# A fused attention and Mish kernel: its head written into the step list, and its first loads cut differently

## The chip, the cores and the metric

The kernel runs on one core of one Trainium2 chip. The metric is device time in microseconds (us), the median of several executions. A core has five engines that run side by side and wait for each other through semaphores: TensorE (PE; its weight loads are listed as PEld) multiplies matrices into PSUM, VectorE (DVE), ScalarE (ACT) and GpSimd (POOL) compute elementwise, and SyncE (SP) issues transfers. ScalarE can issue transfers too. In the profile, "SPq" and "ACTq" are issues of transfers. A program for this core is one list of instructions per engine, each executed in the order in which the kernel's code issued them.

## The reference, cut to what matters

```python
x  = A_x                              # 1 x 2048 x 512, bf16
xn = layernorm(x)                     # over the last axis, no scale or shift
# A: linear attention, 32 heads of 16
q, k, v = split(xn @ wqkv)
pq, pk = q @ w_phi[h], k @ w_phi[h]   # per head, 16 x 16
phi(p) = concat(softmax(p), softmax(-p))
kv = sum_s phi(pk)[s] x v[s];   z = sum_s phi(pk)[s]
o = (phi(pq) @ kv) / (phi(pq) . z + 1e-6)
# B: an MLP
h = xn @ w1 + b1                      # 512 -> 1792
B = (h * tanh(softplus(h))) @ w2      # Mish, 1792 -> 512
out = x + o @ wo + B
```

## The kernel before

The 2048 rows are 16 tiles of 128, in four groups of four. All of x, of the normalised and transposed xn (`xnT`), and of the activated hidden layer (`acts`) stay in SBUF.

The work is cut into named steps, and the order in which the steps are issued is written out by hand in the string `PLAN` (lines 20 to 76). `step(name)` (line 606) takes a name such as `unit_0_7` apart and issues its instructions. So `PLAN` sets the order on every engine at once. A trailing number of some steps picks the engine: for copies out of PSUM (names that end in `=`) 0 is ScalarE and 1 VectorE; for `apply` 0 is VectorE and 2 ScalarE; for `sums` 0 is VectorE and 1 GpSimd. What the names mean:

- `spread_t` (L184), `gather_g` (L189), `root_g` (L202 to L207, GpSimd): statistics of tile t, mean and variance of group g, and 1/sqrt of the variance. `apply_t` (L219, L224) normalises tile t. `turned_t` (L240) turns tiles t and t+1 by a transposing DMA from SP into `xnT`.
- `value_t` and `logits_s_i` (L250, four 128x512 matmuls each): tile t times the value weights; tile i of group s times the folded key weights `wkp` (s below 4) or query weights `wqp` (s from 4 on). Their copies out of PSUM are `value=`, `logits=` and, for the negated query logits, `minus=`. `fold_j` (L164) is a block of the weight product wqkv x w_phi, from `wT`, the transposed weight that a DMA brings (`wq`, L158), and `Wbd`, w_phi as a block diagonal (L550).
- `plane_s_p` (L336 to L344, VectorE): the logits of group s less their row maximum (p = 0) or minimum less the logits (p = 1), both needed before `exp_s_i` (L353, ScalarE); `sums` (L363, L367), `normal_s_k` (L409 to L414, tiles 2k and 2k+1) finish the softmaxes of the keys; `add_s_i` (L427, eight matmuls of 66 columns) sums phi(k) x v; `kv` masks the total. `shift`, `weigh`, `turn`, `attend`, `divide`, `out` do the same for the queries, with DMA transposes (`turn`, `out`).
- `unit_g_f` (L265, four matmuls): block f of the hidden layer for group g; `unit=` (L275) is its Mish on ScalarE, straight from PSUM. It needs `b1f`, the bias turned by TensorE.
- `second_t_n`, `project_t` (L500, L509), `residual_t` (L517), `store_t`: the second layer, the output projection, the sum with x and the store.
- `w2`, `wo`, `wq`: loads of weights.

PSUM has eight banks of 128x512 fp32. `bank(name)` (L125) hands out a bank in turn from a pool; a bank is given again when the step that read it is done. Pool `ps` has six. In the head the function alternates between `ps` and a second pool `hd` of two banks, which is closed behind the head; the two banks later hold the sum of `add`, and then the results of `attend`.

In front of `PLAN` stands the head, written out in lines 524 to 599. The loads are issued first (L524 to L533): on SP tiles 0 and 1 of x, the transposed key weight, tiles 4 to 7, the value weights, all of w1, tiles 8 to 15; on ScalarE's queue w_phi, tiles 2 and 3, the bias. GpSimd builds the identity and the masks. TensorE runs eleven warming matmuls on the identity. Then, for group 0, the statistics come tile by tile, with the square root on ScalarE (`deviate`, L194) and the reciprocal on VectorE (`invert`, L198); TensorE turns the four tiles (`turn_pe`, L233), folds the key weights (L164), and multiplies (L250). Everything of the head is issued before the first step of `PLAN`, `spread_4`; the engines run from the one into the other without a stop.

Of the kernel before, what the change touches and what calls it, by code (L numbers as in the profile page):

```python
# [22 lines left out]
unit_0_5 spread_9 unit=_0_11 spread_11 unit_0_1 unit=_0_5 apply_7_0 apply_6_0 apply_4_2 unit_0_0
spread_10 turned_6 unit=_0_1 unit_0_6 apply_5_0 plane_0_1 unit=_0_0 turned_4 unit_0_9 unit=_0_6
unit_0_10 unit=_0_9 value_0 unit=_0_10 w2 gather_2 value_7 spread_15 root_2 spread_12 logits_1_2
exp_0_2 value=_0_1 value_6 spread_13 exp_0_3 logits_1_0 apply_8_0 apply_11_0 exp_0_0 apply_9_0
unit_0_4 apply_10_0 turned_8 value=_7_1 sums_0_2_1 logits=_1_2_0 unit_1_4 value=_6_0 sums_0_0_0
turned_10 exp_0_1 logits_1_1 gather_3 logits_1_3 logits=_1_0_0 sums_0_1_0 unit_0_2 root_3 sums_0_3_0
value_5 unit=_0_4 unit=_1_4 normal_0_0 unit_1_9 unit=_0_2 unit_2_1 logits=_1_1_0 logits=_1_3_0
unit_2_5 unit=_1_9 apply_12_0 unit_1_6 value=_5_0 plane_1_0 apply_15_2 add_0_0 unit_2_0 apply_14_2  # L30
logits_2_2 unit=_1_6 turned_14 unit=_2_1 unit_1_13 plane_1_1 logits=_2_2_0 wo unit=_2_5 unit_2_3
unit=_1_13 add_0_1 logits_2_1 unit=_2_3 unit=_2_0 value_4 normal_0_1 value_11 exp_1_3 logits_2_3
logits_2_0 apply_13_2 logits=_2_1_1 sums_1_3_1 exp_1_0 add_0_3 turned_12 value=_4_1 add_0_2 unit_1_8
value=_11_1 exp_1_2 logits=_2_0_1 unit_2_12 exp_1_1 sums_1_0_0 value_10 sums_1_2_1 logits=_2_3_0
sums_1_1_0 unit_1_10 unit_1_7 normal_1_0 unit=_1_8 unit_1_5 unit=_2_12 unit_0_13 value=_10_0
unit=_1_7 unit_1_1 plane_2_0 unit=_1_10 unit_2_4 unit=_1_1 unit=_0_13 unit_2_10 unit=_1_5 unit_1_11
unit=_2_10 plane_2_1 unit=_2_4 unit_3_2 wq unit=_1_11 unit_3_5 unit=_3_2 logits_3_1 unit=_3_5
logits_3_3 normal_1_1 add_1_0 logits_3_2 exp_2_2 logits_3_0 exp_2_1 logits=_3_1_1 unit_3_4
logits=_3_0_0 sums_2_1_1 logits=_3_2_1 exp_2_3 unit_3_0 sums_2_2_0 unit_1_0 logits=_3_3_0 sums_2_3_0
exp_2_0 add_1_1 add_1_3 unit_0_8 masks sums_2_0_0 value_15 normal_2_1 unit=_3_4 add_1_2 unit_2_9  # L40
unit=_3_0 unit=_1_0 unit_3_10 unit=_0_8 value_14 value=_15_0 plane_3_0 unit=_2_9 value_8 value=_14_0
add_2_2 value=_8_0 unit_3_11 unit=_3_10 fold_0 unit=_3_11 fold_3 fold_1 unit_2_13 plane_3_1
fold=_0_0 fold=_3_0 unit_1_3 unit=_2_13 unit_0_12 fold=_1_0 unit=_1_3 value_9 unit=_0_12 normal_2_0
fold_2 value_12 value_13 exp_3_3 unit_3_9 value=_9_1 exp_3_1 sums_3_3_1 value=_12_1 unit_3_6
fold=_2_1 exp_3_2 add_2_3 add_2_0 add_2_1 exp_3_0 sums_3_2_0 unit_2_11 unit_2_6 sums_3_1_1
value=_13_1 sums_3_0_0 unit_3_8 unit=_3_9 unit_1_2 unit=_2_6 normal_3_1 unit=_3_6 logits_4_1
unit=_2_11 unit_3_3 logits=_4_1_0 unit=_3_8 logits_4_0 minus=_4_1_1 unit=_1_2 normal_3_0 unit_3_12
logits=_4_0_0 unit_2_7 unit=_3_12 minus=_4_0_0 unit_2_2 unit=_3_3 shift_4_0 logits_5_3 unit=_2_2
unit=_2_7 logits_4_3 logits=_5_3_0 logits_4_2 logits=_4_3_0 logits_5_2 logits=_4_2_1 minus=_5_3_1
add_3_0 add_3_3 exp_4_0 add_3_2 add_3_1 unit_3_13 exp_4_1 kv sums_4_0_1 unit_1_12 logits=_5_2_0  # L50
sums_4_1_0 minus=_4_3_0 logits_5_0 minus=_5_2_0 minus=_4_2_1 unit_3_1 weigh_0 unit_3_7 unit=_3_13
logits_6_1 logits=_5_0_0 shift_4_1 turn_0_0 unit=_1_12 logits_5_1 minus=_5_0_0 logits_6_0 turn_0_1
logits=_6_1_0 unit=_3_1 logits_6_2 unit=_3_7 shift_5_1 logits_6_3 minus=_6_1_0 logits=_5_1_0
unit_2_8 logits=_6_2_0 logits=_6_0_0 second_0_0 minus=_5_1_0 minus=_6_0_0 shift_5_0 second_1_0
exp_4_3 attend_0_0 second_0_1 exp_4_2 divide_0_0 sums_4_3_1 minus=_6_2_0 logits_7_3 logits=_6_3_0
sums_4_2_0 out_0_0 attend_0_1 minus=_6_3_0 logits_7_0 divide_0_1 second_1_1 weigh_1 out_0_1
unit=_2_8 logits_7_1 shift_6_1 turn_1_0 second_2_0 exp_5_2 turn_1_1 exp_5_1 project_0 exp_5_0
second_2_1 residual_0 sums_5_1_1 exp_6_2 sums_5_0_0 project_1 attend_1_0 residual_1 logits_7_2
divide_1_0 store_1 second_3_0 logits=_7_2_0 weigh_2 logits=_7_3_0 out_1_0 minus=_7_3_0 attend_1_1
second_3_1 exp_6_3 shift_6_0 turn_2_1 logits=_7_0_0 second_4_0 minus=_7_0_0 turn_2_0 logits=_7_1_0  # L60
exp_5_3 second_5_0 divide_1_1 minus=_7_2_0 sums_5_3_1 exp_6_1 sums_5_2_0 project_2 out_1_1
minus=_7_1_0 second_5_1 residual_2 shift_7_1 attend_2_1 second_7_0 project_3 weigh_3 second_8_0
exp_7_2 exp_6_0 second_4_1 divide_2_1 turn_3_0 sums_6_0_1 residual_3 turn_3_1 attend_2_0 second_9_0
divide_2_0 sums_6_3_0 out_2_0 second_10_0 sums_6_2_1 sums_6_1_0 store_0 attend_3_0 store_3
second_7_1 divide_3_0 out_2_1 weigh_4 attend_3_1 store_2 project_4 out_3_0 second_9_1 residual_4
turn_4_0 weigh_5 project_5 turn_4_1 divide_3_1 second_8_1 turn_5_1 shift_7_0 second_6_0 turn_5_0
attend_4_0 second_6_1 out_3_1 residual_5 exp_7_1 divide_4_0 second_10_1 exp_7_3 sums_7_1_1 out_4_0
exp_7_0 attend_4_1 project_6 divide_4_1 second_14_0 sums_7_0_0 out_4_1 sums_7_3_1 attend_5_0 weigh_6
project_7 second_14_1 residual_7 turn_6_0 project_8 sums_7_2_1 divide_5_0 second_12_0 turn_6_1
residual_8 attend_5_1 out_5_0 project_9 divide_5_1 second_11_0 weigh_7 out_5_1 attend_6_0  # L70
second_11_1 residual_9 turn_7_1 divide_6_0 second_13_0 store_8 turn_7_0 project_10 out_6_0
attend_6_1 project_11 divide_6_1 second_12_1 residual_10 out_6_1 residual_6 attend_7_0 store_10
second_13_1 divide_7_0 store_4 out_7_0 project_12 attend_7_1 store_6 project_13 divide_7_1 store_9
second_15_0 store_7 residual_13 out_7_1 project_14 store_5 store_13 second_15_1 residual_14
# [5 lines left out]
def kernel(  # L80
# [148 lines left out]
    def turn_pe(t, copy):  # L229
        xn, i = xn_of[0], t  # L230
        ptr = bank("ptr", BF16)
        for kt in range(KT):
            nc.tensor.transpose(  # L233
                ptr[:, kt * P : (kt + 1) * P], xn[:, i, kt * P : (kt + 1) * P], ident[:]
            )
# [326 lines left out]
    for _ in range(11):
        nc.tensor.matmul(
            warm[:].rearrange("p (k c) -> p k c", k=4), lhsT=ident[:], rhs=ident[:, None, :].to_broadcast([P, 4, P]),
            start=True, stop=True,
        )

    for t in (0, 1):
        spread(t)
        gather(t, 1)  # L570
        deviate(t, 1)
    for t in (0, 1):
        invert(t, 1)
        apply(t, nc.vector)
    turn_pe(0, act)
    spread(2)
    spread(3)
    gather(2, 2)
    for kt in (0, 1):
        act(wkp[:, kt, :], fold(wT, kt)[:])  # L580
    deviate(2, 2)
    for kt in (2, 3):
        (dve if kt == 2 else act)(wkp[:, kt, :], fold(wT, kt)[:])
    turn_pe(1, dve)
    invert(2, 2)
    apply(2, nc.vector)
    apply(3, nc.vector)
    logits_copy(0, 0, project(wkp, 0), act)
    p1 = project(wkp, 1, kts=range(0, 2))
    turn_pe(2, dve)  # L590
# [126 lines left out]
```

## Time and profile before

| what | value |
|---|---|
| time, three runs | 177.01, 177.47, 177.53 us; median 177.47 |
| the profiled execution's own time | 177.59 us |
| its span on the core | 175.8 us |
| TensorE's last matmul ends | 172.2 us |
| ScalarE's table loads | 15 of 1.28 us (seven for exp, seven for Mish, one in the head) |
| instructions | 2806 |

The page gives each engine's busy time, a strip of 40 slices of the span (each digit tenths of a slice), and the chain of waits, which is followed back from the last instruction: at each step to what released it. Other views are lists of waits, a timeline (start, duration, engine, line, operation, result and operands, count, and in brackets the idle time in front and what ended it), and the transfers of a window by queue (q1 is SP's, q10 ScalarE's; packets, MB, share of the 16 transfer engines). A busy matmul row contains the time in which its results drain, so rows of neighbours overlap; what a matmul costs in a row of many is the distance of the starts. Some matmul records are missing from a trace, so counts in rows can be lower than what was issued.

### The profile page before, as it was taken

The page shows a single profiled execution, that of the slowest core. Times are in us where ns is not written, and L with a number is a line of the kernel's source. Part 1 is how long each engine was busy: PE and PEld are TensorE (multiplying, and loading weights), DVE is VectorE, ACT ScalarE, POOL GpSimd, SP SyncE. Part 2 cuts the span into 40 slices and gives each one's busy share as a digit, 9 for nine tenths or more (in the row PEclk, how much of TensorE's full clock was granted, in tenths as well). Part 3 has the DMA queues.
Part 4 walks back from the last instruction along what each step waited for, and adds up shares of the span by engine and source line. Part 5 has one row for each costly group of instructions (what it writes and reads, how often), then busy time and mean ns, then how long its engine had stood idle before and what let it go on. Part 6 is the DMA issues. An engine that isn't in the chain of part 4 may idle for free.

```text
span 175.8 us, 2806 instructions
## 1 busy us (share of the span) xinstructions
PE 168.4 (96%) x1021; PEld 82.3 (47%) x1038; DVE 151.6 (86%) x265; ACT 117.3 (67%) x168; POOL 49.3 (28%) x95
## 2 busy tenths in 40 slices
PE   6999987999999999999999999999999999999992
PEld 2444433444544454545445445444445444454571
DVE  0987899999999999998997999999998997973563
ACT  3667999898999899999999999969340006000000
POOL 4201217300550072028005006060528007910000
PEclk9999999999999999999999999999999999999999
DMA  5998089607260000000000311435616584556565
GB/s 145 285 407 305 0 173 355 129 14 171 47 132 0 0 4 0 0 2 4 0 0 0 78 45 30 91 88 127 58 28 148 141 200 85 83 126 163 130 130 179
DMA packets 44618, 18.03 MB, mean 103 GB/s; under 512 B 37052, under 2 KB 44092, under 8 KB 44604
## 3 DMA queue, kind: packets, MB, share of 16 engines
q1 hardware_dynamic: 43632, 17.50, 40.3%
q10 hardware_dynamic: 972, 0.35, 0.8%
q8 instruction: 8, 0.13, 0.3%
q14 instruction: 6, 0.05, 0.1%
HBM read 6.84 MB, written 2.10 MB: 51 GB/s over the span
## 4 chain that ended last, share of the span: by engine, by line
PE 80%; DVE 7%; DMA 7%; SPq 3%; issue 1%
PE po L500 27%; PE ph L265 22%; PE pproj L250 18%; PE po L509 8%; DMA x_sb<-in_A_x_dram 7%; DVE stats L184 2%; PE pkv L427 2%; PE pnd L464 2%; DVE xn L224 2%; SPq L158 2%; DVE m L336 1%; DVE e L344 1%; DVE vext L257 1%; PE pfold L164 1%; DVE x_sb L517 0%
## 5 line engine op out<-in xcount | busy, mean ns | idle before, releaser
L265 PE MATMUL ph<-xnT,w_sb 128*128 128x512 bf16 x224 | 51.6, 379 | 0.0
L500 PE MATMUL po<-w_sb,acts 128*128 128x512 bf16 (+1 forms) x231 | 51.3, 366 | 0.3
L353 ACT ACTIVATE e<-e 128x1024 bf16<-128x1024 bf16 x28 | 28.2, 1051 | 18.2 <-DVE e L323 18.2
L275 ACT ACTIVATE acts<-ph,b1f 128x512 bf16<-128x512 f32 x56 | 35.7, 694 | 1.6 <-PE ph L265 1.2
L367 POOL TENSOR_TENSOR t<-e 128x512 f32<-128x512 bf16 x13 | 15.4, 1187 | 68.2 <-ACT e L353 68.2
L500 PEld LDWEIGHTS <-acts 128*128 128x128 bf16 x238 | 22.7, 98 | 23.6
L265 PEld LDWEIGHTS <-w_sb 128*128 128x128 bf16 x224 | 21.3, 98 | 24.8 <-DMA w_sb<-in_B_w_dram 0.4
L250 PE MATMUL pproj<-wkv,xnT 128*128 128x512 bf16 x121 | 30.2, 379 | 2.0 <-DVE vext L257 1.2
L250 PEld LDWEIGHTS <-xnT 128*128 128x128 bf16 x192 | 18.1, 98 | 23.5 <-issue 2.2
L363 DVE TENSOR_REDUCE sums<-e 128x64 f32<-128x1024 bf16 x15 | 17.9, 1209 | 1.2 <-ACT e L353 1.2
L367 POOL TENSOR_TENSOR t<-t 128x256 f32<-128x256 f32 (+1 forms) x30 | 16.9, 564 | 2.3
L509 PE MATMUL po<-wqk,ob 128*128 128x512 bf16 (+1 forms) x67 | 16.4, 366 | 0.1
L250 PE MATMUL pproj<-wqk,xnT 128*128 128x512 bf16 x62 | 15.3, 379 | 0.1
L184 DVE BATCH_NORM_STATS2 stats<-x_sb 128x6 f32<-128x512 bf16 x16 | 10.2, 679 | 5.3 <-DMA x_sb<-in_A_x_dram 5.3
L517 DVE TENSOR_TENSOR x_sb<-po,x_sb 128x512 bf16<-128x512 f32 (+1 forms) x17 | 10.9, 654 | 2.0 <-PE po L509 1.9
L479 DVE RECIPROCAL r<-pnd 128x32 f32<-128x32 f32 x16 | 5.6, 352 | 7.3 <-PE pnd L464 7.3
L480 DVE TENSOR_TENSOR ob<-pnd,r 128x512 bf16<-128x512 f32 x16 | 11.1, 691 | 0.6
L414 DVE TENSOR_TENSOR e<-e,r 128x2048 bf16<-128x2048 bf16 x8 | 9.8, 1225 | 0.3
L353 ACT ACT_TABLE_LOAD x7 | 9.0, 1283 | 0.7 <-DVE e L323 0.3
L275 ACT ACT_TABLE_LOAD x7 | 9.0, 1283 | 0.1
L509 PEld LDWEIGHTS <-ob 128*128 128x128 bf16 x68 | 6.0, 97 | 5.9 <-DMA ob<-ob 0.5
L285 ACT CAST p<-pproj 128x512 bf16<-128x512 f32 x12 | 6.8, 579 | 2.2 <-PE pproj L250 2.2
(79 smaller groups left out, 184.4 us busy)
## 6 DMA issues: line engine op xcount, KB each, us to landing
w_sb<-in_B_w_dram SPq DMA_DIRECT2D x2, 1792.0 KB, 8.6
out_dram<-x_sb SPq DMA_DIRECT2D x15, 128.0 KB, 1.8
x_sb<-in_A_x_dram SPq DMA_DIRECT2D x1, 1024.0 KB, 11.6
x_sb<-in_A_x_dram SPq DMA_DIRECT2D x1, 512.0 KB, 4.1
wkv<-in_A_wqkv_dram SPq DMA_DIRECT2D x1, 512.0 KB, 4.7
wqk<-in_A_wo_dram SPq DMA_DIRECT2D x1, 512.0 KB, 4.0
x_sb<-in_A_x_dram SPq DMA_DIRECT2D x1, 256.0 KB, 3.1
x_sb<-in_A_x_dram ACTq DMA_DIRECT2D x1, 256.0 KB, 3.5
```

The source lines that it names most:

```text
L184: nc.vector.bn_stats(ln_of[g][0][:, t % TPG, :], x_sb[:, t, :])
L250: nc.tensor.matmul(pp, lhsT=xnT[:, t, kt, :], rhs=w[:, kt, :], start=(kt == 0), stop=(kt == KT - 1),)
L265: nc.tensor.matmul(ph[:], lhsT=w1_sb[:, kt, f * P : (f + 1) * P], rhs=xnT[:, g * TPG : (g + 1) * TPG, kt, :], start=(kt == 0), stop=(kt == ...
L275: nc.scalar.activation(acts[:, f, g * 512 : (g + 1) * 512], ph[:], ACT.Mish, bias=b1f[:, f : f + 1])
L353: nc.scalar.activation(v, v, ACT.Exp)
L363: nc.vector.reduce_sum(out, part, axis=AX.X)
L367: nc.gpsimd.tensor_tensor(out=to[:], in0=part[:, :, 0:n], in1=part[:, :, n : 2 * n], op=ALU.add)
L414: nc.vector.tensor_tensor(out=vv, in0=vv, in1=r2[:, :, None, :].to_broadcast([P, 128, 8, 2]), op=ALU.mult)
L480: nc.vector.tensor_tensor(out=o_t.rearrange("p (u v g d) -> p u v g d", u=2, v=4, g=4), in0=nd[:, :, :, 0:64].rearrange("p u v (g d) -> p ...
L500: nc.tensor.matmul(po[:, c], lhsT=acts[:, f, t * P : (t + 1) * P], rhs=w2_sb[:, f, c], start=(f == 0), stop=False,)
L509: nc.tensor.matmul(po[:, c], lhsT=oT_of[h][:, 2 + t % 2, j * P : (j + 1) * P], rhs=wo_sb[:, j, c], start=False, stop=(j == 3),)
L517: nc.vector.tensor_tensor(out=y, in0=po[:, c], in1=y, op=ALU.add)
```

## The change

The head is no longer written out behind the loads. Its parts become steps (`mean`, `deviate`, `invert`, `flip`, `foldk`, `first`, `bias` and their copies), and `PLAN` is replaced by another order in which they stand among all the others: 577 steps instead of 521, with the same work in total; `first_i_kt` is one matmul of tile i, so four of them make up a tile's logits of group 0. The new order also picks other engines for some steps: of the key logits' copies 11 are on ScalarE and 5 on VectorE (12 and 4 before, the head's included), of the folded key weights' copies all four on ScalarE (three before), of the query logits' copies 14 and 2 (15 and 1), of the `sums` 18 on VectorE and 14 on GpSimd (17 and 15). The places where ScalarE goes from exp to Mish or back, at each of which it loads a table, are 10 instead of 14.

The second PSUM pool of the head is gone: all of it uses the six banks of `ps`. The warming matmuls are nine instead of eleven. The loads: SP brings tile 0 of x alone and then the transposed key weight; ScalarE's queue brings tiles 1 to 3 in one transfer first, then w_phi and the bias; w1 comes in two halves of 896 columns (blocks 0 to 6 and 7 to 13).

The diff, cut to its core; of the plans, the beginning of the old one and the first part and the last lines of the new one:

```diff
 PLAN = """
-spread_4 spread_7 spread_6 value_3 spread_5 plane_0_0 value_1 value_2 value=_1_0 value=_3_0
-value=_2_0 unit_0_7 gather_1 unit_0_3 root_1 spread_8 unit=_0_7 unit_0_11 spread_14 unit=_0_3
...
+spread_0 mean_0 spread_3 deviate_0_1 spread_2 mean_3 mean_2 spread_1 deviate_2_2 invert_0_1
+invert_2_2 mean_1 apply_3_0 deviate_1_1 foldk_0 foldk_1 apply_2_0 foldk=_0_0 flip_3 invert_1_1
+flip_2 apply_0_0 foldk_2 foldk=_1_0 flip=_3_1 flip_0 foldk_3 apply_1_0 flip=_2_0 first_3_0 flip=_0_1
+flip_1 foldk=_2_0 first_2_0 spread_7 first_3_1 flip=_1_0 first_2_1 spread_6 first_3_2 first_0_0
+foldk=_3_0 first_1_0 spread_4 first_0_1 first_2_2 first_1_1 spread_5 first_3_3 first_1_2
+logits=_0_3_0 bias first_0_2 gather_1 first_1_3 first_0_3 root_1 logits=_0_1_1 first_2_3
+logits=_0_0_0 value_2 bias= logits=_0_2_1 unit_0_3 value=_2_1 unit_0_6 unit=_0_3 apply_6_0 apply_4_0
+apply_7_2 unit_0_5 plane_0_0 apply_5_2 turned_6 unit_0_10 unit=_0_5 value_1 unit=_0_10 turned_4
+unit=_0_6 unit_0_12 plane_0_1 unit_0_11 unit=_0_12 value=_1_0 value_3 w2 unit=_0_11 logits_1_2
+value=_3_0 value_7 spread_9 spread_12 value_4 exp_0_2 spread_11 logits_1_0 spread_10 logits=_1_2_0
+sums_0_2_1 spread_14 value_6 value=_7_0 spread_15 value=_4_0 logits_1_1 exp_0_0 spread_8 logits_1_3
+gather_2 logits=_1_0_0 sums_0_0_0 value=_6_0 root_2 value_0 exp_0_1 spread_13 unit_1_12
+logits=_1_3_1 exp_0_3 unit_1_4 gather_3 sums_0_1_0 logits=_1_1_0 root_3 unit_1_11 value=_0_0
+sums_0_3_0 unit_0_8 unit_1_1 unit=_1_12 apply_12_0 apply_8_0 unit_1_8 unit=_1_4 apply_9_0 apply_10_0
+turned_8 unit=_0_8 apply_11_0 unit_1_9 apply_14_0 unit=_1_11 plane_1_0 unit_0_7 unit=_1_8 wo
+unit=_1_1 unit_0_1 turned_10 apply_15_2 unit_1_0 unit=_0_7 turned_14 unit_1_7 unit=_1_9 normal_0_0
+unit=_0_1 unit_1_3 unit=_1_7 unit_1_6 unit=_1_0 apply_13_2 unit_1_13 plane_1_1 unit=_1_6 turned_12
+logits_2_1 unit=_1_3 unit=_1_13 add_0_0 value_5 logits_2_3 normal_0_1 exp_1_2 logits_2_0
+logits=_2_1_0 add_0_1 logits_3_2 logits=_2_3_0 exp_1_1 logits=_2_0_1 sums_1_2_1 logits_2_2
+value=_5_0 add_0_2 logits=_2_2_1 add_0_3 exp_1_0 unit_3_12 sums_1_1_0 unit_3_9 exp_1_3 sums_1_0_0
...
+divide_7_0 residual_11 out_7_0 project_12 attend_7_1 store_9 project_13 divide_7_1 store_11
+second_15_0 store_2 out_7_1 project_14 store_7 second_15_1 residual_14 residual_13 residual_12
+store_13 project_15 store_12 store_14 residual_15 store_15
 """
...
-    turns = [cycle([ps])]
-
+    
     def bank(name, dtype=FP32):
-        return next(turns[0]).tile([P, 512], dtype, name=name, tag="mm")
+        return ps.tile([P, 512], dtype, name=name, tag="mm")
...
-    nc.sync.dma_start(x_sb[:, 0:2, :], x_v[:, 0:2, :])
+    nc.sync.dma_start(x_sb[:, 0, :], x_v[:, 0, :])
+    held = {"wT": load_turned(D)}
+    nc.scalar.dma_start(x_sb[:, 1:4, :], x_v[:, 1:4, :])
     with nc.allow_non_contiguous_dma(reason="tiny w_phi load"):
         nc.scalar.dma_start(wsrc[:], wphi_v)
-    wT = load_turned(D)
-    nc.scalar.dma_start(x_sb[:, 2:4, :], x_v[:, 2:4, :])
     nc.scalar.dma_start(b1b[:], b1_v[:, :])
     nc.sync.dma_start(x_sb[:, 4:8, :], x_v[:, 4:8, :])
     nc.sync.dma_start(wv, wqkv_v[:, :, 2 * D : 3 * D])
-    nc.sync.dma_start(w1_sb[:], w1_v[:, :, :])
+    for c in (slice(0, F // 2), slice(F // 2, F)):
+        nc.sync.dma_start(w1_sb[:, :, c], w1_v[:, :, c])
     nc.sync.dma_start(x_sb[:, 8:16, :], x_v[:, 8:16, :])
...
     warm = bank("warm")
-    for _ in range(11):
+    for _ in range(9):
...
+        elif kind == "mean":
+            gather(n[0], 1)
+        elif kind == "deviate":
+            deviate(*n)
+        elif kind == "invert":
+            invert(*n)
+        elif kind == "flip":
+            held[key] = turn_pe(*n)
+        elif kind == "flip=":
+            copies[alt](xnT[:, n[0], :, :], held.pop(key))
+        elif kind == "foldk":
+            held[key] = fold(held["wT"], *n)
+        elif kind == "foldk=":
+            copies[alt](wkp[:, n[0], :], held.pop(key)[:])
+        elif kind == "first":
+            i, kt = n
+            held["logits", 0, i] = project(wkp, i, held.get(("logits", 0, i)), range(kt, kt + 1))
```

More of the change, by code (lines that the diff above doesn't have):

```diff
@@ L20 @@
 PLAN = """
-spread_4 spread_7 spread_6 value_3 spread_5 plane_0_0 value_1 value_2 value=_1_0 value=_3_0
-value=_2_0 unit_0_7 gather_1 unit_0_3 root_1 spread_8 unit=_0_7 unit_0_11 spread_14 unit=_0_3
[L23 to L74, printed above, removed]
@@ L75 @@
-residual_11 residual_12 store_11 project_15 store_14 store_12 residual_15 store_15
+spread_0 mean_0 spread_3 deviate_0_1 spread_2 mean_3 mean_2 spread_1 deviate_2_2 invert_0_1
[3 more added lines that the diff above has]
+foldk=_3_0 first_1_0 spread_4 first_0_1 first_2_2 first_1_1 spread_5 first_3_3 first_1_2
@@ new lines @@
+logits_2_1 unit=_1_3 unit=_1_13 add_0_0 value_5 logits_2_3 normal_0_1 exp_1_2 logits_2_0
+logits=_2_1_0 add_0_1 logits_3_2 logits=_2_3_0 exp_1_1 logits=_2_0_1 sums_1_2_1 logits_2_2
+value=_5_0 add_0_2 logits=_2_2_1 add_0_3 exp_1_0 unit_3_12 sums_1_1_0 unit_3_9 exp_1_3 sums_1_0_0
+masks unit_1_5 logits=_3_2_0 sums_1_3_0 unit_1_2 unit_3_1 normal_1_0 unit=_3_12 wq unit=_3_9
+unit_0_0 unit=_1_5 unit_2_11 unit=_3_1 logits_3_1 unit=_1_2 plane_2_0 unit_0_4 logits=_3_1_0
+unit=_2_11 logits_3_3 unit=_0_0 unit_2_9 unit=_0_4 normal_1_1 logits_3_0 unit=_2_9 logits=_3_3_0
@@ new lines @@
+add_1_0 unit_1_10 unit_2_6 plane_2_1 unit=_1_10 unit_2_2 unit=_2_6 logits=_3_0_0 add_1_2 fold_1
+unit=_2_2 add_1_3 fold_2 add_1_1 fold=_2_0 fold_3 unit_2_3 plane_3_0 fold=_1_0 fold=_3_0 unit_0_2
+unit=_2_3 unit_2_8 unit=_0_2 unit_3_13 unit=_2_8 plane_3_1 value_14 unit=_3_13 value_8 value_12
+exp_2_3 value_13 value=_12_1 exp_2_1 sums_2_3_1 value=_14_1 value_9 value=_13_1 exp_2_2 value_10
+value=_8_1 exp_3_3 value_15 sums_2_2_0 value=_9_0 fold_0 sums_2_1_1 value_11 exp_2_0 fold=_0_1
+value=_10_1 unit_3_6 value=_15_0 normal_2_1 exp_3_1 unit_3_5 unit_0_13 exp_3_2 unit_3_0 exp_3_0
@@ new lines @@
+value=_11_1 unit_3_2 sums_3_0_1 sums_2_0_0 add_2_2 unit_2_13 unit=_3_6 normal_2_0 add_2_3 unit=_3_5
+unit_3_7 unit=_0_13 unit_2_1 unit=_3_0 unit=_2_13 logits_4_2 unit=_3_2 sums_3_1_0 sums_3_2_1 add_2_1
+unit=_3_7 logits_4_1 unit=_2_1 sums_3_3_0 add_2_0 unit_3_8 logits=_4_2_0 normal_3_0 logits=_4_1_0
+logits_4_3 unit=_3_8 logits_4_0 logits=_4_3_0 minus=_4_2_0 unit_3_3 logits=_4_0_0 normal_3_1
+unit_2_5 minus=_4_1_0 unit=_3_3 unit_2_0 minus=_4_3_0 minus=_4_0_0 unit_2_10 unit=_2_5 shift_4_0
+unit_3_10 unit=_2_0 unit=_2_10 unit_3_11 unit=_3_10 add_3_0 unit=_3_11 add_3_3 logits_5_1 shift_4_1
@@ new lines @@
+logits_5_3 exp_4_0 add_3_1 add_3_2 logits_5_2 exp_4_1 unit_3_4 logits=_5_3_1 logits=_5_1_0
+sums_4_1_1 unit_2_4 exp_4_2 minus=_5_1_1 logits=_5_2_1 unit_2_7 exp_4_3 minus=_5_3_1 unit_0_9
+minus=_5_2_1 sums_4_2_1 sums_4_0_0 unit_2_12 unit=_3_4 logits_6_2 sums_4_3_0 unit=_2_4 logits_6_3
+unit=_0_9 weigh_0 unit=_2_7 logits_6_0 logits=_6_2_0 logits_6_1 logits=_6_3_0 weigh_1 turn_0_1
+unit=_2_12 logits_5_0 minus=_6_2_0 minus=_6_3_0 turn_0_0 logits_7_1 kv logits=_6_0_0 logits_7_0
+minus=_6_0_0 turn_1_0 shift_5_1 logits=_5_0_0 second_0_0 logits=_6_1_0 turn_1_1 minus=_6_1_0
@@ new lines @@
+attend_0_1 minus=_5_0_0 logits_7_2 divide_0_1 second_0_1 exp_5_3 shift_6_0 second_1_0 logits=_7_1_0
+minus=_7_1_0 attend_0_0 second_2_0 divide_0_0 exp_6_0 second_1_1 shift_5_0 logits=_7_0_0 out_0_0
+logits=_7_2_0 minus=_7_0_0 attend_1_0 out_0_1 logits_7_3 second_3_0 logits=_7_3_0 shift_6_1 exp_5_2
+project_0 exp_6_1 second_3_1 exp_5_0 residual_0 exp_5_1 sums_5_0_1 second_2_1 divide_1_0
+minus=_7_2_0 exp_6_2 sums_5_1_0 out_1_0 project_1 exp_6_3 attend_1_1 sums_6_0_0 second_4_0
+sums_6_1_1 minus=_7_3_0 residual_1 second_5_0 weigh_2 project_2 divide_1_1 turn_2_0 sums_5_2_1
@@ new lines @@
+second_5_1 residual_2 out_1_1 sums_5_3_0 second_7_0 turn_2_1 weigh_3 second_6_0 shift_7_0 turn_3_1
+second_4_1 turn_3_0 attend_2_0 second_8_0 store_0 divide_2_0 exp_7_1 project_3 weigh_4 exp_7_0
+out_2_0 second_6_1 sums_6_3_0 sums_7_0_1 turn_4_1 attend_2_1 second_8_1 divide_2_1 second_7_1
+residual_3 out_2_1 sums_6_2_0 sums_7_1_1 turn_4_0 attend_3_1 project_4 divide_3_1 second_9_0
+residual_4 out_3_1 attend_3_0 store_3 second_9_1 divide_3_0 weigh_5 out_3_0 project_5 attend_4_0
+second_10_0 residual_5 turn_5_0 divide_4_0 second_11_0 weigh_6 out_4_0 attend_4_1 turn_5_1 project_6
@@ new lines @@
+divide_4_1 second_11_1 store_5 shift_7_1 turn_6_0 attend_5_0 project_7 out_4_1 second_10_1 turn_6_1
+divide_5_0 exp_7_3 project_8 residual_7 exp_7_2 out_5_0 attend_5_1 residual_8 second_13_0 sums_7_2_1
+divide_5_1 project_9 sums_7_3_0 out_5_1 attend_6_0 second_13_1 residual_6 divide_6_0 store_6 store_8
+project_10 weigh_7 store_4 store_1 second_14_0 turn_7_0 second_12_0 turn_7_1 attend_6_1 second_12_1
+divide_6_1 out_6_0 residual_10 out_6_1 project_11 residual_9 attend_7_0 second_14_1 store_10
@@ L227, in apply, with turn_pe @@
         )
-    def turn_pe(t, copy):
-        xn, i = xn_of[0], t
+    def turn_pe(t):
         ptr = bank("ptr", BF16)
@@ L233, in turn_pe @@
             nc.tensor.transpose(
-                ptr[:, kt * P : (kt + 1) * P], xn[:, i, kt * P : (kt + 1) * P], ident[:]
+                ptr[:, kt * P : (kt + 1) * P], xn_of[0][:, t, kt * P : (kt + 1) * P], ident[:]
             )
-        copy(xnT[:, t, :, :], ptr[:].rearrange("p (k c) -> p k c", k=KT))
+        return ptr[:].rearrange("p (k c) -> p k c", k=KT)
     def turn_dma(t):
@@ L556 @@
     dve, act = nc.vector.tensor_copy, nc.scalar.copy
-    head = ExitStack()
-    hd = head.enter_context(tc.tile_pool(name="hd", bufs=2, space=PSUM))
-    turns[0] = cycle([hd, ps, ps, ps, hd, ps, ps, ps])
     warm = bank("warm")
-    for _ in range(11):
+    for _ in range(9):
         nc.tensor.matmul(
@@ L566 @@
         )
[L568 to L590, printed above, removed]
-    logits_copy(0, 1, project(wkp, 1, p1, kts=range(2, 4)), act)
-    turn_pe(3, act)
-    pb = bank("pb", BF16)
-    nc.tensor.transpose(pb[:, 0:FT], b1b[:], ident[0:FT, 0:FT])
-    nc.vector.tensor_copy(b1f[:], pb[:, 0:FT])
-    for i in range(2, TPG):
-        logits_copy(0, i, project(wkp, i), act)
-    head.close()
-    turns[0] = cycle([ps])
     kvp = ExitStack()
     later = []
-    held = {}
     copies, sides = (act, dve), (nc.vector, nc.gpsimd, nc.scalar)
@@ L608, in step @@
         kind, *n = name.split("_")
-        alt = int(n.pop()) if kind in ("apply", "value=", "logits=", "fold=", "sums", "minus=") else 0
+        alt = int(n.pop()) if kind in ("apply", "value=", "logits=", "fold=", "sums", "minus=", "flip=", "foldk=") else 0
         n = tuple(int(c) for c in n)
@@ L613, in step @@
             spread(*n)
+        elif kind == "mean":
[15 more added lines that the diff above has]
+            held["logits", 0, i] = project(wkp, i, held.get(("logits", 0, i)), range(kt, kt + 1))
+        elif kind == "bias":
+            held[key] = bank("pb", BF16)
+            nc.tensor.transpose(held[key][:, 0:FT], b1b[:], ident[0:FT, 0:FT])
+        elif kind == "bias=":
+            nc.vector.tensor_copy(b1f[:], held.pop(key)[:, 0:FT])
         elif kind == "gather":
```

## The prediction

> **What bounds the kernel now.** I read the page's busy rows and slices first, then the chain of waits, then the list of TensorE's waits, then the timeline of the first 50 us. The page and the chain:
>
> ```profile
> PE 168.4 (96%) x1021; PEld 82.3 (47%) x1038; DVE 151.6 (86%) x265; ACT 117.3 (67%) x168; POOL 49.3 (28%) x95
> ...
> PE   6999987999999999999999999999999999999992
> ...
> 49.44 8.63 PE ph L265 x40
> ...
> 171.73 0.47 PE po L509 x4
> 172.20 0.03 issue
> 172.23 0.42 DVE x_sb L517
> ```
>
> TensorE is the bound. From 31 to 172.2 us the chain is nearly all TensorE; only slices 5 and 6 (22 to 31 us) and the ends are not full. Forty 512-column matmuls take 8.63 us, so one takes 0.216 us. TensorE's waits and the rows around them:
>
> ```profile
> PE warm L563 <- POOL eps L537: 1.4, 1, 1.4
> PE pproj L250 <- DVE vext L257: 1.2, 1, 1.2
> PE pproj L250 <- DMA xnT<-xn: 0.4, 1, 0.4
> PE pfold L164 <- DMA wT<-in_A_wqkv_dram: 0.2, 1, 0.2
> ```
>
> ```profile
> 1.43 4.82 PE L563 MATMUL warm<-ident 128*128 128x512 bf16 x11 [1.43 <-POOL eps L537]
> 6.22 0.40 PE L233 MATMUL ptr<-ident,xn 128*128 128x128 bf16 x4
> 6.87 1.07 PE L164 MATMUL pfold<-Wbd,wT 128*128 128x128 bf16 x16 [0.25 <-DMA wT<-in_A_wqkv_dram]
> ...
> 15.23 7.94 PE L265 MATMUL ph<-xnT,w_sb 128*128 128x512 bf16 x36
> ...
> 24.43 3.63 PE L250 MATMUL pproj<-wkv,xnT 128*128 128x512 bf16 x16 [0.40 <-DMA xnT<-xn]
> 27.89 1.89 PE L265 MATMUL ph<-xnT,w_sb 128*128 128x512 bf16 x8
> 30.99 1.89 PE L250 MATMUL pproj<-wkv,xnT 128*128 128x512 bf16 x8 [1.21 <-DVE vext L257]
> ```
>
> By start times with 0.216 us for each matmul: value_0 should have ended at 23.88, the next group starts at 24.43 (0.55 lost); the eight matmuls from 27.89 end at 29.62, the next start is 30.99 (1.37 lost). That is 1.9 us of waiting in the body. The first projections (logits of group 0) end three value tiles before 15.23: 15.23 - 12 x 0.216 = 12.64.
>
> **TensorE's work behind that point** is the same steps in both plans: units 224 x 0.216 = 48.4; second layer 48.4 (the 256-column ones at half); output projection 13.8; values 64 x 0.216 = 13.8; logits of the other seven groups 112 x 0.216 = 24.2; 16 `add` and 16 `attend` at 0.256 ("0.51 pkv x16" in the chain) 8.2; query folds 0.9. Sum 157.7. Check: 12.64 + 157.7 + 1.9 = 172.2, where the chain leaves TensorE; 3.6 us of last addition and store follow, 175.8, the span. The profiled run took 177.59, 1.79 more; the median shown, 177.47, is 0.12 below it. So the time on the median's scale is (end of first projections) + 157.7 + (later waits W) + 3.6 + 1.67, and the change can move only the first term, W, and the tail.
>
> **Head, part by part.** (1) *Loads.* In the windows of the DMA view the SP queue moved 211 packets of 1 KB by 3.0 us and the ACT queue's first packets come after 2.5:
>
> ```profile
> q1 hardware_dynamic: 115, 0.12, 72.9%
> q10 hardware_dynamic: 66, 0.00, 7.2%
> ...
> 3.96 0.69 DVE L184 BATCH_NORM_STATS2 stats<-x_sb 128x6 f32<-128x512 bf16 x1 [3.96 <-DMA x_sb<-in_A_x_dram]
> ```
>
> (the two queue rows are the window 2.5 to 3.0). Tile 0 alone is 128 packets, so it is here at about 3.2 instead of 3.96. Tiles 1 to 3 (384 KB) start 0.52 us earlier on ACT's queue than tiles 2 and 3 did, which landed at 1.32 + 3.5 = 4.8; I take 4.5, bounds 4.2 and 5.0. w_phi goes second on ACT, behind 384 KB: landing 5.0 to 5.3 instead of 4.1, and Wbd (1.15 us on GpSimd) is ready by 6.5, hidden by the transposed weight wT, which lands at 6.87 as before; without that cover each tenth is a tenth on the path.
> (2) *VectorE.* From 4.5: three statistics at 0.62, the small steps at 0.1 to 0.15, apply of tile 3 (0.41): 7.4. Then applies 2, 0 and 1 and two copies of 0.42: free at 9.4.
> (3) *TensorE.* Folds 0 and 1 at 6.87 (0.22 each), flips 3 and 2 from 7.5, folds 2 and 3 and flip 0 until 8.8, first_3_0 at 8.83 when ScalarE has wkp 0 (deviate_1 at 7.15, copy until 8.0), flip 1, then 15 more matmuls and the bias from 9.27: end at 12.5. The weight copies (0.5 apart on ScalarE) come by 8.5, 9.5 and 10.6 and are in time. Floor: 6.87 + 5.3 of work = 12.15. So the head gives 0.14 (bounds -0.3 and +0.5): two spare PSUM banks are gone (six for all), but each reuse in this stretch is 0.2 or more behind its release.
> (4) *w1 in halves*: units 3 and 6 need the first half at 13.4; all of w1 landed at 15.2 before, half of its bytes are earlier. Unit 10 is the first of the second half, at 16.0: covered by 0.8. One more issue costs SP 0.5 us in front of x tiles 8 to 15, first read at 21 instead of 18.1: nothing.
>
> **Body, by sums over each queue.** Nine tiles (three values, six units) follow the head: TensorE reaches logits_1_2 at 12.5 + 9 x 0.864 = 20.3. It needs tiles 6 and 7 turned. apply_7 is on ScalarE behind unit=_0_3: 14.25 + 1.28 table + 0.6 + 0.83 = 17.0. The turning DMA took 3.2 us with free engines: 20.2. Bounds of this wait: 0, and 1.0 if it waits until x tiles 8 to 15 have landed (18.05 + 3.2). Only 14 packets moved between 17.0 and 18.2, so I take 0.1.
> VectorE is the tight queue from there: from 9.4, four statistics, gather, four copies, two applies: 15.2; two planes (2.95 each) 21.1; seven statistics, gather 25.9; three sums (1.2), a statistic, a copy, a gather 31.3; six applies (0.4) 33.7; plane, normal (2.45), plane 42.05; normal 44.5. This gates ScalarE: exp_1_2 starts at 42.05, and with a table load (1.3), two exps (0.97) and three copies (0.5) value_5 has left its bank at 46.8. unit_3_9, six tiles later, wants that bank at 12.5 + 38 x 0.864 + 1.0 = 46.3: a wait of 0.5. add_0_2 at 45 has its normal at 44.5. Bounds of this group of waits: 0 (VectorE's rows in the stretch 25 to 35 us are up to 0.05 shorter per step) and 1.9 (each of some 45 instructions at its mean instead of start to start, 0.04 more). Behind 47 us the sums leave more room: kv is due on VectorE at 101 against attend_0_1 at 104.3; the tail has the same steps behind attend_7_1 and three residuals before the last one, as before: nothing.
> ScalarE loads its tables for exp and Mish 10 times instead of 14 (4 x 1.28 = 5.1 us less). It is off the path in both, so this counts nothing; it is cover.
>
> **Sum**: W = 0.1 + 0.5 = 0.6 instead of 1.9. 12.5 + 157.7 + 0.6 + 3.6 + 1.67 = **176.1 us**, 1.4 below 177.47. With W from 0 to 1.9 and the head from 12.15 to 12.95 this case reaches from 175.2 to 177.2.
>
> **Rivals.** *A, the old waits only change their place*: the turning waits for the load (1.0) and the bank for VectorE (1.0), W = 2.0: 177.5, no change. For it: VectorE is 100% busy from 22 to 35 us in the trace and gets no less to do. Against: the sums show it at most 0.5 late.
> *B, TensorE's array is still slow in the head.* The eleven warming matmuls ran at 0.427 us spacing (4.82 us), the same shape later at 0.216, though the granted clock reads 1.00 throughout; the last of them took 574 ns instead of 634, so the switch came at about 6.15. With nine they end at 5.5, and TensorE then idles until 6.87. If the switch then comes one more such stretch later, at about 9.6, the 2.4 us of work placed in 6.9 to 9.6 gets half done: 1.0 us on the path, 177.1. For it: the switch in the trace came only just after the work that is now cut. Against: 4.0 us of activity stand before the hole.
> The Trainium skill (TensorE: Matmul & The Clock Gate, Part 1: The HAM clock gate) has this as a gate that opens after a window of about 3.4 us of sustained activity, the windows running free of the kernel's start, and that closes after an idle window; the trace agrees with the factor of two. By that page the hole of 1.4 us doesn't close the gate, but a window that contains it may fail to open it, which is rival B.
> *C, slower.* VectorE falls behind for good before 45 us. Place: the six applies of tiles 8 to 14 and what stands behind them. Before, four of these took 2.69 us while GpSimd ran sums beside them (one at 1.03 us instead of 0.41). If the new order runs all of them beside GpSimd, that is six at 0.65: 1.6 more; with the 1.9 of the bound above, value_5's bank is 3.5 late: W = 4.0 at most, about 3.2 where the two overlap: 178.7. It decides from 1.3 us of lag on. Against: GpSimd's own sum puts root_3 at an end of 30.7 and nothing until exp_1_2.
> *D, the change doesn't do what it says*: tile 0 isn't early because ACT's transfer shares the engines. Then VectorE starts at 3.9, is through tile 0 by 4.6, and still waits for nothing else than tiles 1 to 3: 0.1, inside the range.
>
> **Chances.** Forecast (with D) 0.62, A 0.16, B 0.09, C 0.13. A measurement here tells a change from 0.3% (0.53 us) on: faster is below 176.94, slower above 178.0. The forecast is below 176.94 in nine of ten of its cases, B in four, A in one or two: faster 0.62. C is slower nearly always, A in one of ten: 0.14. Same: 0.24. The range takes in A and B and leaves out most of C: 175.2 to 177.9.
>
> **What would show it.** Right: first statistics at about 3.2, first fold at 6.9, first unit at about 13.4, no wait on vext of 1.2 us, TensorE's list with less than 1 us of waits after 12.5, ten table loads, TensorE's last matmul near 170.8. Rival A: a wait of 1 us on xnT<-xn near 20 or on a bank near 46. B: 219 ns folds replaced by about 270 or more. C: VectorE's second normal later than 46 and a wait of over 2 us near it. The prediction is wrong if tiles 1 to 3 land after 5.3, or if a wait appears behind 50 us, where I only summed queues.

## The result and the profile after

| | before | after |
|---|---|---|
| median | 177.43 us (20 runs, 177.00 to 177.92) | 176.62 us (20 runs, 175.26 to 177.49) |
| ratio | | 0.9941, 95% interval 0.9918 to 0.9963 |
| profiled execution, span | 177.59, 175.8 us | 176.83, 175.1 us |

The new kernel is 0.6% faster. Its times lie in two groups: 8 of 20 runs between 175.26 and 175.76, none between 175.8 and 176.3, and 12 between 176.31 and 177.49. Before, all lie within 0.9 us. The profiled execution is one of the second group. The chain of the page before, then rows of its own page, and the list of TensorE's waits:

```profile
PE 80%; DVE 7%; DMA 7%; SPq 3%; issue 1%
```

```profile
PE 168.3 (96%) x1020; PEld 84.2 (48%) x1036; DVE 151.6 (87%) x267; ACT 111.3 (64%) x163; POOL 47.9 (27%) x91
...
PE   6799999999999999999999999999999999999992
...
PE 94%; DMA 3%; issue 1%; DVE 0%; SPq 0%
```

```profile
PE warm L565 <- POOL eps L542: 1.4, 1, 1.4
PE pfold L169 <- DMA wT<-in_A_wqkv_dram: 1.2, 1, 1.2
```

The 8 and the 7 that stood in the slices from 22 to 31 us have become 9s, and the waits on `vext` and `xnT` are gone; the chain is 94% TensorE where it was 80%. (The new 7, near 5 us, is the wait for `wT` in the head.) So the body's 1.9 us of waits were removed whole. The time they set free came only in part, and the timeline of the head shows why:

```profile
1.43 4.02 PE L565 MATMUL warm<-ident 128*128 128x512 bf16 x9 [1.43 <-POOL eps L542]
...
3.29 0.69 DVE L189 BATCH_NORM_STATS2 stats<-x_sb 128x6 f32<-128x512 bf16 x1 [3.29 <-DMA x_sb<-in_A_x_dram]
...
4.49 1.29 DVE L189 BATCH_NORM_STATS2 stats<-x_sb 128x6 f32<-128x512 bf16 x2 [0.30 <-DMA x_sb<-in_A_x_dram]
...
6.69 1.04 PE L169 MATMUL pfold<-Wbd,wT 128*128 128x128 bf16 x8 [1.23 <-DMA wT<-in_A_wqkv_dram]
...
9.65 0.63 PE L254 MATMUL pproj<-wkv,xnT 128*128 128x512 bf16 x1
...
14.69 3.62 PE L269 MATMUL ph<-xnT,w_sb 128*128 128x512 bf16 x16
```

The loads land where they were expected (3.29 and 4.49 us). But eight folds take 1.04 us, about 0.107 from start to start, and a 512-column matmul at 9.65 takes 0.63 us: the array runs at half speed until about 10.2. The first unit starts at 14.69 instead of the 13.4 of the prediction's own head. This is rival B, in this execution.

### The profile page after: what moved, and what is told of

It is laid out like the page before. It is cut to its first block, busy times and chain, and to the rows that moved or that the text cites. A ratio compares the mean times of both kernels' runs of the same rounds, so it can differ in the third digit from the quotient of the medians.

```text
span 175.1 us, 2806 instructions
## 1 busy us (share of the span) xinstructions
PE 168.3 (96%) x1020; PEld 84.2 (48%) x1036; DVE 151.6 (87%) x267; ACT 111.3 (64%) x163; POOL 47.9 (27%) x91
## 4 chain that ended last, share of the span: by engine, by line
PE 94%; DMA 3%; issue 1%; DVE 0%; SPq 0%
PE ph L269 28%; PE po L504 27%; PE pproj L254 24%; PE po L513 8%; DMA wT<-in_A_wqkv_dram 3%; PE pnd L468 2%; PE pkv L431 2%; PE pfold L169 2%; PE ptr L237 1%; DVE x_sb L521 0%; SPq L528 0%; PE pb L601 0%
## 5 line engine op out<-in xcount | busy, mean ns | idle before, releaser
L269 PE MATMUL ph<-xnT,w_sb 128*128 128x512 bf16 x224 | 50.6, 379 | 0.0
L254 PE MATMUL pproj<-wkv,xnT 128*128 128x512 bf16 x123 | 29.7, 381 | 0.3
L367 DVE TENSOR_REDUCE sums<-e 128x64 f32<-128x1024 bf16 x16 | 18.9, 1207 | 0.4 <-ACT e L357 0.4
L371 POOL TENSOR_TENSOR t<-t 128x256 f32<-128x256 f32 (+1 forms) x28 | 15.8, 564 | 2.2
L306 ACT CAST e<-pproj 128x512 bf16<-128x512 f32 x12 | 6.9, 605 | 2.8 <-DMA qT<-e 1.6
L468 PEld LDWEIGHTS <-qT 128*128 128x128 bf16 x128 | 6.2, 97 | 3.8
L289 ACT CAST p<-pproj 128x512 bf16<-128x512 f32 x11 | 6.3, 585 | 2.1 <-PE pproj L254 2.1
```

The source lines that it names most:

```text
L254: nc.tensor.matmul(pp, lhsT=xnT[:, t, kt, :], rhs=w[:, kt, :], start=(kt == 0), stop=(kt == KT - 1),)
L269: nc.tensor.matmul(ph[:], lhsT=w1_sb[:, kt, f * P : (f + 1) * P], rhs=xnT[:, g * TPG : (g + 1) * TPG, kt, :], start=(kt == 0), stop=(kt == ...
L367: nc.vector.reduce_sum(out, part, axis=AX.X)
L371: nc.gpsimd.tensor_tensor(out=to[:], in0=part[:, :, 0:n], in1=part[:, :, n : 2 * n], op=ALU.add)
```

## The experiments

Each kernel was timed on one chip together with the kernel before; ratios are to that, with their 95% intervals. The kernel before had medians from 177.3 to 177.7 us on these chips, so rows of different experiments are compared by their ratios.

### The number of warming matmuls

```diff
-    for _ in range(9):
+    for _ in range(12):
```

Four kernels change this number in the new kernel (w6, w11, w12, w14), one in the kernel before (b9, nine instead of eleven).

> The new kernel with 12 warming matmuls instead of 9, nothing else. Theory (rival B came true in part of the executions: the array's slow phase ends at a boundary that runs free of the kernel, and the idle stretch from 5.45 to 6.7 us lets a boundary pass without opening): at 0.427 us each the twelve end at about 6.55, the idle stretch is gone, the slow phase ends at the latest near 8.3 us, so the runs lie closer together, between 175.2 and 176.4 instead of 175.26 to 177.49, median 175.6 (1.0 below before). Against: if the spread of the new kernel comes from elsewhere (transfers, the order of the steps), the runs keep their spread of 2 us and the median stays near 176.6.

> The new kernel with 6 warming matmuls instead of 9. Theory: they end at 4.2 us, TensorE idles for 2.5 us, nearly every boundary before 8 us has too little work behind it, and the switch comes at 9.5 to 12 us in nearly all executions: folds at about 290 ns or more in the profile, median 177.2 or more, the group near 175.5 gone or rare. Rival (the spread comes from elsewhere): the same distribution as with 9, median about 176.6.

> The new kernel with 11 warming matmuls, as many as before. Theory: they end at 6.3 us, the idle stretch before the first fold is 0.4 us, nearly all windows are full: median 175.3 to 175.8, like 12. Rival (any idle stretch before the folds can spoil the switch): two groups of times as with 9, median above 176.

> The new kernel with 14 warming matmuls. Theory: if the slow phase lasts through them they end at 7.4 us, 0.7 behind the first fold's data, but the switch lies between 4.8 and 8.3 us and those behind it run at half the price, so the loss is 0 to 0.5: median 175.4 to 175.8 where 12 gave 175.4, spread under 1.2 us. Rival (more warming goes on helping because the switch is still late in some executions with 12): 175.2 or less. Rival (each one costs its 0.43): 176.2.

> The kernel before with 9 warming matmuls instead of 11. Theory: its first real work on TensorE begins at 6.22 and its idle stretch grows from nothing to about 0.8 us; some executions switch a window later, which costs them up to 1 us: median 177.6 to 178.0, spread wider than the 0.9 us of before. Rival (nine are enough, two are dead weight): the same times as before, 177.4.

| kernel | warming matmuls | runs, us | median | ratio |
|---|---|---|---|---|
| w6 | 6 | 12, 176.94 to 178.09 | 177.36 | 1.0010 (0.9994 to 1.0027) |
| after | 9 | 20, 175.26 to 177.49 | 176.62 | 0.9941 (0.9918 to 0.9963) |
| w11 | 11 | 5, 175.05 to 175.73 | 175.32 | 0.9885 (0.9867 to 0.9903) |
| w12 | 12 | 6, 175.17 to 176.04 | 175.36 | 0.9892 (0.9869 to 0.9915) |
| w14 | 14 | 6, 175.12 to 176.17 | 175.24 | 0.9885 (0.9866 to 0.9905) |
| b9, old kernel | 9 | 12, 176.98 to 177.97 | 177.33 | 1.0001 (0.9987 to 1.0016) |

With six, the whole gain of the change is lost and the faster group is gone; with 11 to 14, none of 17 runs is above 176.17. The timeline of w12:

```profile
1.43 5.30 PE L565 MATMUL warm<-ident 128*128 128x512 bf16 x12 [1.43 <-POOL eps L542]
6.65 0.73 PE L169 MATMUL pfold<-Wbd,wT 128*128 128x128 bf16 x8
...
13.30 2.97 PE L269 MATMUL ph<-xnT,w_sb 128*128 128x512 bf16 x13
```

Eight folds now take 0.73 us in all, and the first unit starts 1.39 us earlier than in the profile of nine. This settles that too few warming matmuls made the second group. Idle time between them and the first fold does no harm by itself, once the array is fast. In the profile of switch76, a kernel described further down with twelve warming matmuls, it is nearly as long as with nine, and the folds run at full speed behind it:

```profile
1.43 4.85 PE L565 MATMUL warm<-ident 128*128 128x512 bf16 x12 [1.43 <-POOL eps L542]
7.36 0.62 PE L169 MATMUL pfold<-Wbd,wT 128*128 128x128 bf16 x8 [1.09 <-DMA wT<-in_A_wqkv_dram]
```

The twelve take 4.85 us there and 5.30 in w12, so the array became fast while they were still running. By the starts of single matmuls, it became fast at some point between 4.3 us (switch2, where the twelve take 4.18 us) and 6.9 us (w12) in every profile with eleven or more. Nine end at 5.45 us and six at 4.17. By this nine are enough in some executions and not in others, and six in none; that is an inference, as no execution of the faster group with nine was profiled. More matmuls also leave a shorter idle stretch behind them, and no run tells which of the two counts while the array is slow.

w14's median of 175.24 lies between its theory (175.4 or more) and its first rival (175.2 or less), and its ratio is no different from w11's and w12's; the second rival is out. So eleven are enough here.

b9 fell against its theory: the times are those of the rival, that nine are enough. But nine were not enough in its profile, which shows the slow array too, and what hid it:

```profile
6.71 1.90 PE L164 MATMUL pfold<-Wbd,wT 128*128 128x128 bf16 x16
...
16.52 7.93 PE L265 MATMUL ph<-xnT,w_sb 128*128 128x512 bf16 x36
24.29 4.48 PE L250 MATMUL pproj<-wkv,xnT 128*128 128x512 bf16 x19
28.60 1.89 PE L265 MATMUL ph<-xnT,w_sb 128*128 128x512 bf16 x8
31.04 1.89 PE L250 MATMUL pproj<-wkv,xnT 128*128 128x512 bf16 x8 [0.55 <-DVE vext L257]
```

Sixteen folds take 1.90 us (1.07 before) and the first unit starts at 16.52 instead of 15.23. At 31.04, however, it is level with the kernel before (30.99): the wait on `xnT` is gone and that on `vext` is 0.55 instead of 1.21. In the old order VectorE, which waits 1.31 us for the load of tiles 8 to 15 (at 18.08), sets the pace up to 31 us, and a head 1.3 us late disappears in waits.

### Which part brings the gain

**headnew**: new loads, new head steps (without the others between them), 12 warming matmuls, then the old plan.

```diff
 PLAN = """
+spread_0 mean_0 spread_3 deviate_0_1 spread_2 mean_3 mean_2 spread_1 deviate_2_2 invert_0_1
...
+first_1_3 first_0_3 logits=_0_1_1 first_2_3 logits=_0_0_0 bias= logits=_0_2_1
 spread_4 spread_7 spread_6 value_3 spread_5 plane_0_0 value_1 value_2 value=_1_0 value=_3_0
```

> The new loads and the new head (its steps in their new order, without the others between them, 12 warming matmuls, w1 in halves), then the plan of before unchanged. Theory (the gain is the body's 1.9 us of waits; in the old order the stretch from 18 to 31 us hangs on the load of tiles 8 to 15, which lands at 18 us, and on VectorE behind it, so an earlier head is eaten by longer waits): same as before, 177.0 to 177.4, with TensorE's waits near 24 and 30 us as long as before or longer. Rival (the early loads and the finer head carry the gain): 176.0 or less.

Median 178.52 us, ratio 1.0055 (1.0039 to 1.0072): slower than before. TensorE's waits:

```profile
PE pproj L254 <- DMA xnT<-xn: 1.7, 1, 1.7
...
PE pproj L254 <- DVE vext L261: 1.2, 1, 1.2
```

The first unit starts at 14.77, 0.46 earlier than before, and the wait on `xnT` has grown from 0.4 to 1.7. The place is VectorE's queue, here a row of the kernel before and two of headnew:

```profile
11.02 2.47 DVE L184 BATCH_NORM_STATS2 stats<-x_sb 128x6 f32<-128x512 bf16 x4
...
11.95 0.69 DVE L289 CAST p<-pproj 128x512 bf16<-128x512 f32 x1 [3.27 <-PE pproj L254]
...
13.24 1.27 DVE L189 BATCH_NORM_STATS2 stats<-x_sb 128x6 f32<-128x512 bf16 x2
```

Without the statistics of tiles 4 to 7 between the head's steps VectorE idles 3.27 us in front of a copy, and those statistics begin at 13.24 instead of 11.02. (In the kernel before, ScalarE makes all four copies of these logits; the new head gives two to VectorE.) Part of the 2.2 us goes into the 1.31 us that VectorE waited for tiles 8 to 15 before; the applies of tiles 7 and 6 start 0.75 us later (21.22 instead of 20.47), and TensorE gets `xnT` 0.8 us later (25.23 instead of 24.43). The theory expected 177.0 to 177.4: it had the mechanism (an earlier head is eaten), but not that the head alone can be worse.

**bodynew**: the old head as it was written, with its loads of x, eight banks and eleven warming matmuls; w1 in halves; then the new order without the head's steps.

```diff
-PLAN = """spread_4 spread_7 spread_6 value_3 ...
+PLAN = """spread_7 spread_6 spread_4 spread_5 gather_1 ...
-    nc.sync.dma_start(w1_sb[:], w1_v[:, :, :])
+    for c in (slice(0, F // 2), slice(F // 2, F)):
+        nc.sync.dma_start(w1_sb[:, :, c], w1_v[:, :, c])
```

> The head of before as it was written (its loads of x, eleven warming matmuls, eight banks), w1 in halves, then the new order of all other steps. Theory: first projections end at 12.6 to 12.7 as before, then no waits: 175.5 to 175.9. Rival (the head's steps must lie among the others for the gain): 176.5 or more, with a wait of TensorE between 13 and 31 us.

Median 175.76 us, ratio 0.9900 (0.9884 to 0.9916). The first unit starts at 13.48, and the list of TensorE's waits has one line:

```profile
PE warm L563 <- POOL eps L537: 1.4, 1, 1.4
...
13.48 3.62 PE L264 MATMUL ph<-xnT,w_sb 128*128 128x512 bf16 x16
```

So the new order of the body, with w1 in halves, brings the whole gain that w12 has. Laying the head out among the rest is not needed for it: bodynew and w12 differ by less than their intervals. The halves alone did not bring it in headnew, which has them too. What within the order does it (the sequence, the other engines for some steps, the fewer table loads) was not separated.

**w1whole**: w12 with w1 in one transfer.

> The new kernel with 12 warming matmuls, but w1 in one transfer. Theory: the first unit is due at 13.3 us and all of w1 landed at 15.2 us before, so TensorE waits about 1.9 us there, all of it on the path: 177.1 to 177.4 instead of 175.4. Rival (other work in the queues or an earlier landing hides it): 175.4 to 175.8.

Median 177.12 us, ratio 0.9969 (0.9949 to 0.9989), that is 1.4 us (0.77% of 177.4) worse than w12:

```profile
14.93 3.63 PE L269 MATMUL ph<-xnT,w_sb 128*128 128x512 bf16 x16 [1.45 <-DMA w_sb<-in_B_w_dram]
```

The halves are a condition of the new order: the first unit is due at 13.3, and the undivided transfer ends behind that. The wait came out at 1.45 instead of 1.9, as w1 landed at 14.9.

**xold**: w12 with tiles 0 and 1 of x on SP, tiles 2 and 3 on ScalarE's queue behind w_phi.

> The new kernel with 12 warming matmuls, but x as before: tiles 0 and 1 on SP, tiles 2 and 3 on the ACT queue behind w_phi, in the new order of steps. Theory of the prediction (tiles 1 to 3 at 4.5 instead of 4.8, VectorE's chain sets the flips): 0.3 later, 175.6 to 175.8. Rival (the transposed weight and ScalarE's copies set the head's end): no difference, 175.4.

Median 175.82 us, as the theory said, but on a chip where the kernel before was slower too: the ratio, 0.9897 (0.9881 to 0.9912), can't be told from w12's by the intervals. In the profile TensorE waits 0.27 us for the first normalised tile at 7.54, and the first unit starts at 13.53 instead of 13.30. The new cut of x is worth some 0.2 us by these two profiles, and nothing that the times can show.

### Is ScalarE cover?

switch2 adds to w12 two exponentials of one column, each between two runs of Mish, so that ScalarE loads tables twice more at each; switch53 and switch76 add one of them. What they compute is used by nothing.

```diff
-... logits_3_1 unit=_1_2 plane_2_0 ...
+... logits_3_1 unit=_1_2 switch_209 plane_2_0 ...
-... unit_3_7 unit=_0_13 unit_2_1 ...
+... unit_3_7 unit=_0_13 switch_295 unit_2_1 ...
...
+        elif kind == "switch":
+            nc.scalar.activation(root[:], eps[:], ACT.Exp)
```

> The new kernel with 12 warming matmuls and two one-column exponentials put among the Mish activations (near 53 and 76 us), so that ScalarE loads its tables 14 times again, as before the change. It computes nothing that is used. Theory (ScalarE is cover): 175.3 to 175.7, no difference from the kernel without them. Rival (the new order lives on the four loads it saves, 5.1 us of ScalarE): 176.5 to 180, with TensorE waiting for a bank behind a Mish.

> As switch2, with the one-column exponential near 53 us alone (two more table loads, 12 in all, nothing used). Theory (what a load costs is set by its place: the banks ahead of it are covered here): 175.2 to 175.7, like the kernel without it. Rival (every load of 1.28 us in the stretch up to 100 us ends up on the path): 176.5 to 177.9.

> As switch2, with the one-column exponential near 76 us alone (two more table loads). Theory: TensorE has about 0.9 us before it needs the bank that the next Mish sets free, so of the 2.8 us in ScalarE's queue about 2 show: 177.0 to 177.9, nearly all that switch2 cost, with a wait of 1.5 to 2 us for a Mish near 81 us. Rival (the two places share the cost): 176.2 to 176.8.

| kernel | median, us | ratio |
|---|---|---|
| switch2 (both) | 177.96 | 1.0036 (1.0021 to 1.0052) |
| switch53 | 175.97 | 0.9908 (0.9884 to 0.9931) |
| switch76 | 178.49 | 1.0041 (1.0025 to 1.0058) |

switch2 fell against its theory, and its rival came true: two places with two loads each cost the whole gain. switch53's median lies 0.3 above its theory, but its ratio can't be told from w12's, and its profile has no TensorE wait behind ScalarE. switch76 cost more than was forecast (178.49 against 177.0 to 177.9), and all of what switch2 costs. The wait came as expected, on TensorE and then on ScalarE:

```profile
81.49 1.02 PE L254 MATMUL pproj<-wqk,xnT 128*128 128x512 bf16 x4 [1.66 <-ACT acts L279]
...
74.79 1.28 ACT L279 ACT_TABLE_LOAD   x1
76.08 1.84 ACT L279 ACTIVATE acts<-ph,b1f 128x512 bf16<-128x512 f32 x3
77.94 1.28 ACT L605 ACT_TABLE_LOAD   x1
79.24 0.20 ACT L605 ACTIVATE root<-eps 128x1 f32<-128x1 f32 x1
79.46 1.28 ACT L279 ACT_TABLE_LOAD   x1
```

After eight exps and a load, banks filled by units already wait for their Mish there; 2.8 us more in the queue show as 1.66 and, at 99.77, another 0.29 us of TensorE's time. This profile is of the slowest of switch76's twelve executions (179.74; the others lie between 178.22 and 178.97), in which the first unit is also 0.44 us later than in w12 and a wait on `ob` near the end takes 0.57. switch2's profile (177.77, near its median) is the better measure. Its span is 176.0 us against 173.9 in w12, and it has the same two waits:

```profile
80.88 1.02 PE L254 MATMUL pproj<-wqk,xnT 128*128 128x512 bf16 x4 [1.66 <-ACT acts L279]
...
99.16 5.34 PE L254 MATMUL pproj<-wqk,xnT 128*128 128x512 bf16 x24 [0.29 <-ACT acts L279]
```

With 0.16 us behind a copy of VectorE at 97.18 they make 2.1 us, as much as the spans differ by. By the medians the loads near 76 us cost 2.6 us (1.0041 against 0.9892 is 1.5%); the remaining 0.5 us stays open. So whether a table load costs anything is decided by its place.

## Why the prediction was right, and where it was not

The forecast (176.1, ratio 0.9925) and the measured median (176.62, 0.9941) differ by 0.5 us. That they came so near is in part luck: two errors of the sum, W and rival B below, cancel in part. w12 is the kernel whose profile the sum describes, one in which the array is fast from the first folds on.

- **TensorE's work behind the head, 157.7 us, and its place as the bound**: right. In w12 the first unit starts at 13.30, so the first projections end at 13.30 - 0.86 = 12.44, and TensorE's part of the chain ends at 170.18: 157.74.
- **Head, 12.5**: right without rival B, 12.44. Loads as expected; fold at 6.65. The price of the x loads (0.3 us, as xold's theory drew it from the prediction) was about right by the profiles (0.23), and is too small to be seen in times.
- **W = 0.6**: mis-sized, it is 0 apart from 0.15 on `ob` in w12's tail. The term of 0.5 for value_5's bank rested on a sum over VectorE's queue that ends at 44.5; in w12 the second `normal` ends at 43.51, value_5's copy at 45.27, and unit_3_9 needs the bank at about 46.3. The sum was 1.0 us too long: 0.3 of it stood at its start (VectorE leaves the head's copies at 9.06, not 9.4), and the six applies took 2.0 us instead of 2.4. The term of 0.1 for `turned_6` had a step wrong: the load of the Mish table was put behind the first unit's data. In w12 it starts at 13.06, ahead of its data, and the activation follows at 14.37, so `apply_7` came 1.2 us earlier than 17.0 said.
- **Rival B**: named, with the right mechanism, but held for 0.09. By their times it came true in more than half of the runs (12 of 20 lie above 176.3). Its price of 1.0 us was near: in the profile the first unit is 1.39 late and TensorE's last matmul 1.2 (171.36 against 170.18). The 0.6 us too much in W and the array's 1.2 us in most runs give a median 0.5 above the forecast.
- **Rivals A and C**: neither wait came in any profile of the new order, but for 0.28 us on `xnT` at 21.79 in w6's; VectorE was ahead of the sum, not behind it.
- **w1 in halves, priced at nothing with the cover that was named**: right, and the price without it is 1.4 us.
- **ScalarE's table loads "count nothing"**: true of the old order, which had 14 and no wait of TensorE on ScalarE, and of the new one as it stands. That ScalarE is cover everywhere in the new order is wrong: two more loads near 76 us cost the whole gain, by switch76.
- **The place of the gain**: right. It is the order of the body; bodynew shows that it doesn't hang on the head.

A version that beats both is the new kernel with eleven or more warming matmuls: 0.9885 (0.9867 to 0.9903) with 11, some 2.0 us below before.

## What to carry to other kernels

When TensorE is the bound, first find the waits in its own list, and check whether an earlier stage feeds them: a faster head is worth nothing while a later queue sets the pace, and once those waits are gone every late start in the head is on the path. A warm-up must last until the array is fast, and that moment moves from execution to execution (here 2.9 to 5.5 us after the first matmul, over the profiles with eleven or more); eleven matmuls or more, which reach up to the first real work or to 0.6 us before it, were enough in all 17 runs. One run is not a distribution: where the times fall into two groups, something differs from execution to execution, and one profile shows only one side of it.
